# Attention's normalising in blocks of eight heads instead of four, with buffers by block

## The chip, the cores and the metric

The kernel runs on one core of a Trainium2 chip. The metric is device time in microseconds (us), the median of the runs shown.

## What is computed

The reference chains an attention with sinks and a sliding window and two MLPs, all in float32. Only its core stands here.

```python
# attention: 2 batches, 8 heads, 768 positions, head dimension 64; 4 sinks, window 128
scores = scale * np.matmul(q, k.transpose(0, 1, 3, 2))
keep = is_sink | in_window
scores = np.where(keep, scores, -1e9)
a = np.exp(scores - max(scores))
a = a / (sum(a) + 1e-9)
x = np.matmul(a, v)          # reshaped to 1536 tokens x 512
h = x @ w_in                 # first MLP, 512 -> 2048 -> 512
x = np.where(h > 0, h, np.exp(np.minimum(h, 0)) - 1) @ w_out
h = x @ w2_in                # second MLP
out = (h - np.tanh(h)) @ w2_out
```

## The kernel before

Every operation is first recorded by `Plan` (lines 42 to 400) and then put into an order by a list scheduler, which works with costs and waiting times written into the class. Among operations that are ready on an engine it takes the one with the highest rank. For a kind of work that has an entry in `DUE` (line 62) the rank comes from a due time in us, a first value plus a second one times the number of the group, chunk or step; smaller is earlier. Kinds without an entry are ranked by the length of the work that hangs on them. `PICK` (line 69) says for operations that several engines could do which of them may. `BONUS` is what PE gives for staying in its tile mode, `MARGIN` what another engine must be faster by before an operation is left to it. Where PE would be idle in the schedule's reckoning before the first MLP ends its first step, `idle` (line 588) is put in, a filler matmul that is of no other use. As the order is fixed when the kernel is built, the queues of all engines run in that order. Nearly all instructions carry line 400, several matmuls recorded together line 168, fillers line 591.

Attention works on 12 chunks of 128 positions; six make up one batch. A group is half a chunk's heads, four, so there are 24. In `attention` (line 799) a group runs `scores` twice, for two heads each: PE writes scores into two banks (`b_sc`, two in all), DVE adds the mask and takes the maximum (into `nm_all`), ACT makes exponentials and their sums (`sm_all`). Then `norm` (line 724) adds 1e-9 to the four sums, takes reciprocals and scales the four heads' rows. `sink_T` (line 736) is for chunks that see the sinks apart from their window: it copies the sinks' weights, splits them into a rounded part and a remainder, and transposes them on PE. `pair_T` transposes two heads' weights, and an eviction brings them to `arena`. When both groups of a chunk are done, `PV` (line 771) multiplies by the values and splits the result into `xhi` and `xlo`, which the MLPs read. Rows are 128 columns wide in the first chunk of a batch, 256 in the second, 264 in the other four.

The first MLP begins beside attention, in blocks of 256 tokens with three pieces of its weights (`PHASES`, line 437; each piece has an in and an out half, six halves in all); all later stages work on 512 tokens. `w_split` (line 854) loads a half's 64-bit words, narrows them (line 829) and splits them into a rounded part and a remainder in `w`, by work on ACT, DVE and POOL. Two buffers `raw` serve the loads of the first weights. Loads are issued on SP.

Buffers that the change touches: `r_a` (line 530, weights of attention, three of four heads each), `r_aT` (line 532, transposed pairs, eight), `r_as` and `r_asT` (lines 534 and 535, sinks' weights and their transposes, one and two).

Of the kernel before, what the change touches and what calls it, by code (L numbers as in the profile page):

```python
# [41 lines left out]
class Plan:  # L42
# [16 lines left out]
    BONUS, MARGIN = 2030.75, 5520.33  # L59
# [11 lines left out]
        ("norm", "tensor_scalar", 264, False): ("DVE",), ("T", "copy", 64, False): ("POOL",),  # L71
        ("late w", "tensor_scalar", 512, False): ("DVE",), ("late ew", "tensor_tensor", 512, False): ("DVE",),
        ("T", "tensor_tensor", 32, False): ("DVE",), ("late ew", "copy", 512, False): ("ACT",),
        ("c", "tensor_copy", 128, False): ("POOL",), ("w", "tensor_scalar", 512, False): ("POOL",),
        ("late w", "tensor_tensor", 512, False): ("DVE",), ("late out", "copy", 512, True): ("DVE",),
        ("w", "tensor_tensor", 512, False): ("DVE",), ("T", "copy", 256, True): ("ACT",),
        ("late w", "copy", 512, False): ("DVE",), ("T", "copy", 512, True): ("ACT",),
        ("out", "copy", 512, True): ("ACT",), ("x", "copy", 512, True): ("ACT", "DVE"),
        ("norm", "tensor_scalar", 128, False): ("DVE",), ("norm", "tensor_scalar", 256, False): ("DVE", "POOL"),
        ("w", "copy", 512, False): ("ACT", "DVE", "POOL"), ("z", "copy", 512, False): ("DVE",),  # L80
        ("ew", "tensor_tensor", 256, False): ("DVE",),
# [322 lines left out]
def tile_sink_attention__two_mlps(  # L404
# [52 lines left out]
    def copy(out, in_):  # L457
        ways = [(V_, "tensor_copy"), (S_, "copy")]
        if in_.space != PSUM:
# [21 lines left out]
             F32R: arena_p.tile([P, 2464], F32R, name="arena_r")}  # L481
# [45 lines left out]
    KS, NS, QB, VB, AB, TB = 144, 3, 2, 4, 3, 8  # L527
    r_q = Ring("att", (HP, P), F32, QB)
    slots = carve("att", (NS, HP, KS))
    r_a = Ring("att", (4, KW), F32, AB)  # L530
# [3 lines left out]
    r_as = Ring("att", (3, 4, MAXSINK), F32R)  # L534
    r_asT = Ring("att", (P,), F32R, 2)
# [152 lines left out]
    def scores(g, pr):  # L688
# [4 lines left out]
        if pr == 0:  # L693
            a_t[g] = r_a()
# [16 lines left out]
        for e in range(2):  # L711
            j = place(g, e) + pr
            col = 4 * g + j
            a = a_t[g][:, j, 0:n]
# [9 lines left out]
    def norm(g):  # L724

        plan.tag = ("norm", g)
        n = width((g // 2) % NI)
        r = sm_all[:, 4 * g:4 * g + 4]
        ts(out=r, in0=r, scalar1=1e-9, scalar2=None, op0=ALU.add)
        V_.reciprocal(out=r, in_=r)  # L730
        for j in range(4):
            a = a_t[g][:, j, 0:n]
            plan.either((G_, "tensor_scalar"), (V_, "tensor_scalar"), out=a, in0=a, scalar1=r[:, j:j + 1],
                        scalar2=None, op0=ALU.mult)

    def sink_T(g):
        plan.tag = ("T", g)
        if (g // 2) % NI < 2:
            return
        a = a_t[g][:, :, P:P + MAXSINK]  # L740

        s = r_as()
        copy(s[:, 1:3], a.unsqueeze(1).to_broadcast([P, 2, 4, MAXSINK]))
        sub(None, s[:, 0], a, s[:, 1].bitcast(F32))
        tr = b_tu(P)[0:3 * S4]
        T_.matmul(
            out=tr, lhsT=s.rearrange("p a h s -> p (a h s)").bitcast(F32), rhs=ident,
            is_transpose=True, start=True, stop=True,
        )
        aS_t[g] = r_asT()[0:3 * S4]  # L750
        copy(aS_t[g], tr)

    def pair_T(g, pr):
# [4 lines left out]
        a = a_t[g]  # L758
# [432 lines left out]
```

## Time and profile before

| | us |
|---|---|
| median of 3 runs | 637.05 |
| lowest and highest | 636.72, 637.23 |
| the profiled execution | 636.36 |
| its span, first to last instruction | 634.6 |
| PE busy in it | 627.1 |
| DVE busy | 431.9 |
| ACT busy | 278.6 |
| POOL busy | 30.8 |

The clock granted to PE was 0.998 of full speed in the mean. PE is TensorE's matmuls, PEld its weight loads, DVE VectorE, ACT ScalarE, POOL GpSimd, SP the engine that issues DMAs. The ends of matmuls are modelled and overlap, so a group's mean time is longer than the step from one matmul to the next. A line of the timeline that merges several instructions gives the time from the first start to the last end; an instruction may start before the end that is shown for the one ahead of it.

### The profile page before, as it was taken

The page shows a single profiled execution, that of the slowest core. Times are in us where ns is not written, and L with a number is a line of the kernel's source. Part 1 is how long each engine was busy: PE and PEld are TensorE (multiplying, and loading weights), DVE is VectorE, ACT ScalarE, POOL GpSimd, SP SyncE. Part 2 cuts the span into 40 slices and gives each one's busy share as a digit, 9 for nine tenths or more (in the row PEclk, how much of TensorE's full clock was granted, in tenths as well). Part 3 has the DMA queues.
Part 4 walks back from the last instruction along what each step waited for, and adds up shares of the span by engine and source line. Part 5 has one row for each costly group of instructions (what it writes and reads, how often), then busy time and mean ns, then how long its engine had stood idle before and what let it go on. Part 6 is the DMA issues. An engine that isn't in the chain of part 4 may idle for free.

```text
span 634.6 us, 9256 instructions
## 1 busy us (share of the span) xinstructions
PE 627.1 (99%) x3430; PEld 514.5 (81%) x3430; DVE 431.9 (68%) x1061; ACT 278.6 (44%) x615; POOL 30.8 (5%) x41
## 2 busy tenths in 40 slices
PE   9999999999999999999999999999999999999996
PEld 6677877899888888888888888888888888888885
DVE  6999999999824479943459998367974553423232
ACT  5788887875533345533445453223422222222220
POOL 3631020100000000000000000000000000000000
PEclk9999999999999999999999999999999999999999
DMA  6543444345500122430012243011220000001012
GB/s 212 172 162 121 130 162 133 99 139 165 165 1 0 35 66 68 132 100 0 1 34 67 74 158 116 17 40 59 70 66 2 2 0 1 0 1 66 2 66 72
DMA packets 22005, 47.21 MB, mean 74 GB/s; under 512 B 2240, under 2 KB 9408, under 8 KB 21952
## 3 DMA queue, kind: packets, MB, share of 16 engines
q1 hardware_dynamic: 21952, 46.54, 23.7%
q8 instruction: 29, 0.48, 0.3%
q14 instruction: 24, 0.20, 0.1%
HBM read 43.39 MB, written 3.15 MB: 73 GB/s over the span
## 4 chain that ended last, share of the span: by engine, by line
PE 82%; DVE 13%; DMA 2%; POOL 1%; SPq 1%; issue 1%; ACT 0%; DVEq 0%; POOLq 0%
PE bank L400 79%; DVE arena L400 7%; DVE t L400 3%; PE bank L168 2%; DVE arena_r L400 1%; DVE w L400 1%; DMA raw<-in_moe_w_in_dram 1%; DVE xlo L400 1%; SPq L400 1%; POOL t L400 1%; DMA arena<-in_kq_dram 1%; DVE sm_all L400 1%; POOL arena_r L400 0%; DVE xhi L400 0%; ACT arena L400 0%
## 5 line engine op out<-in xcount | busy, mean ns | idle before, releaser
L400 PE MATMUL bank<-xhi,w 128*128 128x512 f32 (+1 forms) x840 | 250.7, 373 | 0.0
L400 PEld LDWEIGHTS bank<-xhi,w 128*128 128x128 f32 x840 | 154.6, 188 | 28.7 <-issue 1.6
L400 PE MATMUL bank<-arena_r,w 128*128 128x512 f32 (+1 forms) x684 | 158.8, 358 | 0.0
L400 PE MATMUL bank<-w,arena_r 128*128 128x512 f32 (+1 forms) x594 | 154.4, 383 | 0.0
L400 PE MATMUL bank<-xlo,w 128*128 128x512 f32 (+1 forms) x420 | 148.2, 373 | 0.0
L400 ACT CAST arena_r<-arena 128x512 fp32r<-128x512 f32 (+1 forms) x96 | 57.9, 603 | 194.2 <-PE bank L400 192.1
L400 PEld LDWEIGHTS bank<-arena_r,w 128*128 128x128 f32 x684 | 116.5, 189 | 19.3 <-issue 0.9
L400 DVE TENSOR_TENSOR arena_r<-arena,arena_r 128x512 fp32r<-128x512 f32 (+3 forms) x123 | 71.4, 582 | 89.1 <-PE bank L400 42.8
L400 PEld LDWEIGHTS bank<-w,arena_r 128*128 128x128 f32 x594 | 109.3, 188 | 22.1
L400 ACT ACTIVATE arena<-bank 128x512 f32<-128x512 f32 (+1 forms) x105 | 57.9, 560 | 101.0 <-PE bank L400 97.5
L400 PEld LDWEIGHTS bank<-xlo,w 128*128 128x128 f32 x420 | 79.0, 188 | 14.6 <-issue 1.1
L400 DVE TENSOR_TENSOR arena<-bank,arena 128x512 f32<-128x512 f32 (+1 forms) x65 | 42.4, 677 | 38.2 <-ACT arena L400 31.8
L168 PE MATMUL bank<-arena 128*64 128x128 f32 (+3 forms) x544 | 55.3, 327 | 0.5 <-DVE nm_all L400 0.4
L400 ACT ACTIVATE arena<-arena,nm_all 128x264 f32<-128x264 f32 (+2 forms) x96 | 46.8, 491 | 15.6 <-DVE nm_all L400 14.9
L400 DVE SCALAR_TENSOR_TENSOR arena<-arena,bank 128x512 f32<-128x512 f32 (+1 forms) x57 | 33.9, 596 | 22.0 <-ACT arena L400 22.0
L400 ACT ACTIVATE arena<-arena 128x512 f32<-128x512 f32 (+1 forms) x73 | 42.5, 587 | 8.1 <-DVE w L400 6.6
L168 PEld LDWEIGHTS bank<-arena 128*64 128x64 f32 (+1 forms) x544 | 34.7, 154 | 11.1 <-issue 4.3
L400 DVE SCALAR_TENSOR_TENSOR t<-raw,t 128x512 uint32<-128x512 uint32 x54 | 37.2, 688 | 0.2
L400 DVE CUSTOM_DVE_ANT_0 arena<-bank,arena 128x264 f32<-128x264 f32 (+2 forms) x96 | 35.1, 398 | 0.4 <-PE bank L168 0.2
L400 ACT COPY arena<-bank 128x512 f32<-128x512 f32 (+1 forms) x52 | 27.5, 544 | 3.2 <-PE bank L168 3.2
L400 DVE TENSOR_SCALAR t<-t 128x512 f32<-128x512 f32 (+1 forms) x64 | 27.1, 425 | 2.0 <-POOL t L400 1.1
L168 PE MATMUL bank<-ident,arena 128*128 128x128 f32 x176 | 27.6, 281 | 0.2 <-DVE xlo L400 0.2
(67 smaller groups left out, 408.8 us busy)
## 6 DMA issues: line engine op xcount, KB each, us to landing
raw<-in_moe_w_in_dram SPq DMA_DIRECT2D x20, 512.0 KB, 3.7
raw<-in_moe_w_out_dram SPq DMA_DIRECT2D x20, 512.0 KB, 3.8
arena<-in_moe_w_in_dram SPq DMA_DIRECT2D x12, 512.0 KB, 3.6
arena<-in_moe_w_out_dram SPq DMA_DIRECT2D x12, 512.0 KB, 3.6
arena<-in_kq_dram SPq DMA_DIRECT2D x22, 256.0 KB, 3.4
arena<-in_v_dram SPq DMA_DIRECT2D x12, 256.0 KB, 3.4
out_dram<-part SPq DMA_DIRECT2D x8, 256.0 KB, 2.2
out_dram<-arena SPq DMA_DIRECT2D x3, 256.0 KB, 2.5
```

Source lines behind the costliest of these rows:

```text
L168: eng.matmul(**kw)
L400: real(*self.ops[n][3], **self.ops[n][4])
```

## The change

The buffers of attention's weights hold a whole chunk, eight heads, and there are two of them. `norm` and `sink_T` run once a chunk, behind both groups' scores: one addition and one reciprocal for eight sums, then eight scalings; one subtraction for the sinks' weights of both groups, two transposes into one bank recorded together, one eviction. The four `pair_T` and `PV` follow. Transposed pairs have six buffers in place of eight, the transposed sinks one of double size. The constants of the plan are others: due times, the engines that may do an operation, `BONUS` and `MARGIN`.

```diff
--- before.py
+++ after.py
@@ -56,29 +56,31 @@
     TOP = 640e3
     WINDOW, ENOUGH, IDLE = 3413.3, 3100.0, (109.2, 256.0)
     SWITCH = (196.0, 95.0)
-    BONUS, MARGIN = 2030.75, 5520.33
+    BONUS, MARGIN = 10109.72, 5963.27
 
     HOLD = {}
     DUE = {
-        "c": (-2246.58, 70.043), "score": (-751.72, 15.580), "ew": (169.97, 10.912), "lkq": (-825.49, 29.089),
-        "norm": (31.65, 0.041), "lw": (-323.61, 20.339), "w": (-51.16, 95.951), "end": (1519.18, -106.955),
-        "x": (-392.68, 18.828), "pv": (89.97, 9.529), "in": (76.02, 17.601), "out": (207.21, 11.159),
-        "kq": (-189.70, 22.587), "T": (23.13, 10.469), "ok": (444.48, 24.538), "lv": (48.72, 3.987),
+        "c": (-2406.72, -14.630), "score": (-1413.68, 28.549), "ew": (331.51, 0.606), "lkq": (-1382.77, 27.576),
+        "norm": (-507.50, -6.572), "lw": (-1164.05, 68.531), "w": (2009.13, 142.798), "end": (1067.44, -87.300),
+        "pv": (-462.76, 5.811), "in": (81.51, 14.384), "out": (102.53, 20.095), "T": (-367.90, 8.180),
+        "x": (-151.46, 6.200), "z": (192.47, 20.402), "late ew": (-512.87, 6.303), "lv": (-62.63, 13.646),
+        "ok": (4.72, 0.000),
     }
 
     PICK = {
         ("T", "copy", 128, True): ("ACT",), ("ew", "copy", 256, False): ("ACT", "DVE"),
-        ("norm", "tensor_scalar", 264, False): ("DVE",), ("T", "copy", 64, False): ("POOL",),
-        ("late w", "tensor_scalar", 512, False): ("DVE",), ("late ew", "tensor_tensor", 512, False): ("DVE",),
-        ("T", "tensor_tensor", 32, False): ("DVE",), ("late ew", "copy", 512, False): ("ACT",),
-        ("c", "tensor_copy", 128, False): ("POOL",), ("w", "tensor_scalar", 512, False): ("POOL",),
-        ("late w", "tensor_tensor", 512, False): ("DVE",), ("late out", "copy", 512, True): ("DVE",),
-        ("w", "tensor_tensor", 512, False): ("DVE",), ("T", "copy", 256, True): ("ACT",),
-        ("late w", "copy", 512, False): ("DVE",), ("T", "copy", 512, True): ("ACT",),
-        ("out", "copy", 512, True): ("ACT",), ("x", "copy", 512, True): ("ACT", "DVE"),
-        ("norm", "tensor_scalar", 128, False): ("DVE",), ("norm", "tensor_scalar", 256, False): ("DVE", "POOL"),
-        ("w", "copy", 512, False): ("ACT", "DVE", "POOL"), ("z", "copy", 512, False): ("DVE",),
-        ("ew", "tensor_tensor", 256, False): ("DVE",),
+        ("norm", "tensor_scalar", 264, False): ("DVE", "POOL"), ("T", "copy", 64, False): ("ACT", "DVE"),
+        ("late w", "tensor_scalar", 512, False): ("DVE",),
+        ("late ew", "tensor_tensor", 512, False): ("DVE", "POOL"), ("T", "tensor_tensor", 32, False): ("DVE",),
+        ("late ew", "copy", 512, False): ("DVE",), ("c", "tensor_copy", 128, False): ("POOL",),
+        ("w", "tensor_scalar", 512, False): ("POOL",), ("late w", "tensor_tensor", 512, False): ("DVE",),
+        ("late out", "copy", 512, True): ("ACT",), ("w", "tensor_tensor", 512, False): ("DVE",),
+        ("T", "copy", 256, True): ("DVE",), ("late w", "copy", 512, False): ("DVE", "POOL"),
+        ("T", "copy", 512, True): ("ACT",), ("out", "copy", 512, True): ("ACT",),
+        ("x", "copy", 512, True): ("ACT",), ("norm", "tensor_scalar", 128, False): ("DVE",),
+        ("norm", "tensor_scalar", 256, False): ("DVE",), ("w", "copy", 512, False): ("ACT", "DVE"),
+        ("z", "copy", 512, False): ("DVE",), ("ew", "tensor_tensor", 256, False): ("DVE",),
+        ("T", "tensor_tensor", 64, False): ("DVE", "POOL"),
     }
 
     def __init__(self, tc):
@@ -478,7 +480,7 @@
 
 
     arena = {F32: arena_p.tile([P, 14336], F32, name="arena"),
-             F32R: arena_p.tile([P, 2464], F32R, name="arena_r")}
+             F32R: arena_p.tile([P, 2560], F32R, name="arena_r")}
     bank = [banks_p.tile([P, 512], F32, name=f"bank{n}") for n in range(8)]
     top_of = {}
 
@@ -524,15 +526,15 @@
 
     gsA = Ring("att", (2, 256), F32R, 3)
 
-    KS, NS, QB, VB, AB, TB = 144, 3, 2, 4, 3, 8
+    KS, NS, QB, VB, AB, TB = 144, 3, 2, 4, 2, 6
     r_q = Ring("att", (HP, P), F32, QB)
     slots = carve("att", (NS, HP, KS))
-    r_a = Ring("att", (4, KW), F32, AB)
+    r_a = Ring("att", (8, KW), F32, AB)
     masks = carve("att", (4, KW))
     r_aT = Ring("att", (2, 2, P), F32, TB)
     r_v = Ring("att", (H, D), F32, VB)
-    r_as = Ring("att", (3, 4, MAXSINK), F32R)
-    r_asT = Ring("att", (P,), F32R, 2)
+    r_as = Ring("att", (2, 3, 4, MAXSINK), F32R)
+    r_asT = Ring("att", (2, P), F32R, 1)
     r_vsink = Ring("att", (HP, P), F32R)
     eA = Ring("att", (256,), F32, 2)
     part2 = carve("late", (4, 512))
@@ -690,8 +692,8 @@
         plan.tag = ("score", g)
         c, half = divmod(g, 2)
         i, o = c % NI, c % NS
-        if pr == 0:
-            a_t[g] = r_a()
+        if pr == 0 and half == 0:
+            a_t[c] = r_a()
         p = 2 * half + pr
         n = width(i)
         mm, S = [], []
@@ -711,7 +713,7 @@
         for e in range(2):
             j = place(g, e) + pr
             col = 4 * g + j
-            a = a_t[g][:, j, 0:n]
+            a = a_t[c][:, 4 * half + j, 0:n]
             V_.tensor_tensor_reduce(
                 out=a, in0=S[e][:, 0:n], in1=masks[:, mi, 0:n], scale=-SCALE, scalar=3.0e38,
                 op0=ALU.add, op1=ALU.min, accum_out=nm_all[:, col:col + 1],
@@ -721,41 +723,44 @@
                 bias=nm_all[:, col:col + 1], accum_out=sm_all[:, col:col + 1],
             )
 
-    def norm(g):
-
-        plan.tag = ("norm", g)
-        n = width((g // 2) % NI)
-        r = sm_all[:, 4 * g:4 * g + 4]
+    def norm(c):
+
+        plan.tag = ("norm", 2 * c + 1)
+        n = width(c % NI)
+        r = sm_all[:, 8 * c:8 * c + 8]
         ts(out=r, in0=r, scalar1=1e-9, scalar2=None, op0=ALU.add)
         V_.reciprocal(out=r, in_=r)
-        for j in range(4):
-            a = a_t[g][:, j, 0:n]
+        for j in range(8):
+            a = a_t[c][:, j, 0:n]
             plan.either((G_, "tensor_scalar"), (V_, "tensor_scalar"), out=a, in0=a, scalar1=r[:, j:j + 1],
                         scalar2=None, op0=ALU.mult)
 
-    def sink_T(g):
-        plan.tag = ("T", g)
-        if (g // 2) % NI < 2:
+    def sink_T(c):
+        plan.tag = ("T", 2 * c + 1)
+        if c % NI < 2:
             return
-        a = a_t[g][:, :, P:P + MAXSINK]
+        a = a_t[c].rearrange("p (g h) k -> p g h k", g=2)[:, :, :, P:P + MAXSINK]
 
         s = r_as()
-        copy(s[:, 1:3], a.unsqueeze(1).to_broadcast([P, 2, 4, MAXSINK]))
-        sub(None, s[:, 0], a, s[:, 1].bitcast(F32))
-        tr = b_tu(P)[0:3 * S4]
-        T_.matmul(
-            out=tr, lhsT=s.rearrange("p a h s -> p (a h s)").bitcast(F32), rhs=ident,
-            is_transpose=True, start=True, stop=True,
-        )
-        aS_t[g] = r_asT()[0:3 * S4]
-        copy(aS_t[g], tr)
+        for g in range(2):
+            copy(s[:, g, 1:3], a[:, g].unsqueeze(1).to_broadcast([P, 2, 4, MAXSINK]))
+        sub(None, s[:, :, 0], a, s[:, :, 1].bitcast(F32))
+        tr = b_tu(2, P)[0:3 * S4]
+        plan.many([
+            dict(out=tr[:, g], lhsT=s[:, g].rearrange("p a h s -> p (a h s)").bitcast(F32), rhs=ident,
+                 is_transpose=True, start=True, stop=True)
+            for g in range(2)
+        ])
+        t = r_asT()[0:3 * S4]
+        copy(t, tr)
+        aS_t[2 * c], aS_t[2 * c + 1] = t[:, 0], t[:, 1]
 
     def pair_T(g, pr):
 
         plan.tag = ("T", g)
         c = g // 2
         i = c % NI
-        a = a_t[g]
+        a = a_t[c][:, 4 * (g % 2):4 * (g % 2) + 4]
         tr = b_tu(2, 2, P)
         c0, c1 = slice(0, P), slice(P, 2 * P) if i == 1 else s1
         cols = (c1, c0) if i != 1 and c % NS == 0 else (c0, c1)
@@ -810,11 +815,11 @@
                 load_v(c + 1)
             scores(g, 0)
             scores(g, 1)
-            norm(g)
-            sink_T(g)
-            pair_T(g, 0)
-            pair_T(g, 1)
             if half:
+                norm(c)
+                sink_T(c)
+                for k in range(4):
+                    pair_T(2 * c + k // 2, k % 2)
                 PV(c)
```

## Rows read from the trace of the kernel before

**Rows 1.** Busy time by stage: length, then busy us (instructions) per engine, clock, DMA.
```profile
0.00:30.00 30.00, 28.70 (x219) 18.35 (x221) 25.13 (x113) 19.29 (x62) 14.87 (x19) 1.00 0.60 187
30.00:109.00 79.00, 78.82 (x693) 61.60 (x689) 77.71 (x308) 64.87 (x205) 13.97 (x18) 1.00 0.45 142
109.00:152.90 43.90, 43.86 (x402) 40.52 (x403) 43.29 (x131) 32.57 (x83) 2.00 (x4) 1.00 0.45 139
152.90:634.60 481.70, 475.71 (x2122) 394.08 (x2120) 285.82 (x513) 161.90 (x269) 0.00 (x0) 1.00 0.16 50
```

**Rows 2.** Chain that ended last, in order of time: start us, us, engine, tile written.
```profile
108.39 0.61 DVE xlo L400
109.04 0.66 PE bank L168 x4
```

**Rows 3.** Fillers (line 591): all of them, those until 30 us, two windows, one series.
```profile
L591 PE MATMUL bank<-const-bfloat16-1.0 x122: 272/273/418, 0.8 to 40.4; 128*16 128x256 bf16 x122
...
L591 PE MATMUL bank<-const-bfloat16-1.0 128*16 128x256 bf16 x117 | 16.7, 288 | 0.8 <-PEq L1145 0.8
...
10.00:20.00 10.00, 5.29 (x41) 3.18 (x39) 1.00 0.65 221
20.00:30.00 10.00, 4.21 (x29) 2.27 (x29) 1.00 0.55 176
...
17.32 1.83 PE L591 MATMUL bank<-const-bfloat16-1.0 128*16 128x256 bf16 x15
```

**Rows 4.** DVE by time, 50 to 80 us: start us, us, operation, shapes, count.
```profile
52.51 0.16 DVE L400 TENSOR_SCALAR sm_all<-sm_all 128x4 f32<-128x4 f32 x1
52.58 0.41 DVE L400 TENSOR_TENSOR arena_r<-arena,arena_r 128x256 fp32r<-128x256 f32 x1
52.92 0.17 DVE L400 RECIPROCAL sm_all<-sm_all 128x4 f32<-128x4 f32 x1
53.01 0.38 DVE L400 SCALAR_TENSOR_TENSOR arena<-arena,bank 128x256 f32<-128x256 f32 x1
53.31 1.15 DVE L400 TENSOR_SCALAR arena<-arena,sm_all 128x264 f32<-128x264 f32 x4
...
56.62 0.18 DVE L400 TENSOR_TENSOR arena_r<-arena,arena_r 128x32 fp32r<-128x32 f32 x1
56.73 0.68 DVE L400 TENSOR_TENSOR w<-t,w 128x512 fp32r<-128x512 f32 x1
```

**Rows 5.** Groups by shape, DVE until 109 us, last ACT whole span: busy, mean ns.
```profile
L400 DVE SCALAR_TENSOR_TENSOR t<-raw,t 128x512 uint32<-128x512 uint32 x24 | 16.6, 692 | 0.1
L400 DVE TENSOR_SCALAR arena<-arena,sm_all 128x264 f32<-128x264 f32 x48 | 14.3, 348 | 0.0
L400 DVE TENSOR_TENSOR w<-t,w 128x512 fp32r<-128x512 f32 x11 | 7.5, 678 | 0.0
...
L400 DVE TENSOR_SCALAR arena<-arena,sm_all 128x256 f32<-128x256 f32 x9 | 3.6, 431 | 0.0
...
L400 DVE CAST xhi<-bank 128x512 fp32r<-128x512 f32 x3 | 2.0, 681 | 0.0
...
L400 ACT CAST arena_r<-arena 128x512 fp32r<-128x512 f32 (+1 forms) x96 | 57.9, 603 | 194.2 <-PE bank L400 192.1
```

**Rows 6.** Head by time: DVE, then POOL, then PE, between 16 and 32 us.
```profile
16.46 0.69 DVE L400 SCALAR_TENSOR_TENSOR t<-raw,t 128x512 uint32<-128x512 uint32 x1
...
19.09 0.41 DVE L400 CUSTOM_DVE_ANT_0 arena<-bank,arena 128x256 f32<-128x256 f32 x1
...
19.77 0.68 DVE L400 TENSOR_TENSOR w<-t,w 128x512 fp32r<-128x512 f32 x1
...
18.00 3.24 POOL L400 TENSOR_SCALAR arena<-arena,sm_all 128x256 f32<-128x256 f32 x3
...
29.23 2.63 PE L168 MATMUL bank<-arena 128*64 128x128 f32 x36
...
31.88 0.50 PE L400 MATMUL bank<-xhi,w 128*128 128x256 f32 x2
```

## Prediction, made before the changed kernel was run

> **What bounds the kernel now.** I read the busy time by stage first [rows 1]. In it the reader is to see where DVE is full: 25.1 of the first 30 us, 77.7 of the next 79, still full from 109 to 152.9, and 59% (285.8 of 481.7 us) after that. PE looks full in every stage, but ends of matmuls are modelled and fillers count as work, so this column alone decides nothing. The chain that ended last does: in order of time it runs nearly wholly through DVE until 108.39 us, through PE from 109.04 us on [rows 2]. So the time is what the front takes on DVE, plus PE's work from 109 us on, which the change leaves as it is.
>
> Then I ask how much PE really idles in the front, since only that can be won. 117 fillers lie in the first 30 us, 41 of them from 10 to 20 and 29 from 20 to 30 us; 15 in a row take 1.83 us, 0.12 each, so all 117 take 14 us [rows 3]. From 30 to 109 us only 5 fillers are left (122 in all, from the count in [rows 3]), and the better measure is PEld: weight loads are busy 61.6 of 79 us there (78%), against 40.5 of 43.9 (92%) in the stage behind it, where PE never leaves the chain [rows 1]. Were the mix of matmuls the same, PE would idle 79 x (1 - 78/92) = 12 us; the lower bound is the 5 fillers, 0.6 us. I take 5 us. **Ceiling: 14 us in the head, some 5 us after it.**
>
> **The change, part by part.** Terms are of the profiled run (span 634.6 us, 636.36 with what lies around it). That is 0.7 us under the median of 637.05, and I subtract what is saved from the median.
>
> Reciprocals. 24 additions and 24 reciprocals of four columns become 12 and 12 of eight. They last 0.16 and 0.17 us, but on a full engine what counts is when the next instruction starts: the addition at 52.51 is followed at 52.58, the reciprocal at 52.92 at 53.01 [rows 4]. Twelve pairs at 0.16 us are 1.9 us; by the durations, as the upper bound, 12 x 0.33 = 4.0. The four more columns I take at nothing, beside a scaling's 264.
> By the Trainium skill ("VectorE: DVE Perf Modes", section on the TRN2 errata) an instruction carries a fixed term that it measures at about 150 cycles and that is exposed between instructions. An estimate from that page, 24 x 0.156, would make this term 3.7 us. The rows agree with the figure as a duration and disagree as a step from start to start; by the rows it is 1.9.
>
> Sinks' weights. 16 subtractions of 32 columns become 8 of 64. One steps by 0.11 us (56.62 to 56.73 [rows 4]); eight fewer and eight somewhat longer give 0.7 us (0 to 0.9). The 16 transposes stay; the 16 evictions behind them on ACT become 8, off the chain. The 16 copies of 64 columns leave POOL for ACT or DVE: at the same 0.11 us, half of them on DVE, +0.9 us (0 to 1.8). Reciprocals and sinks: when the chain turns to PE at 109 us, 48 of the 64 scalings of full width are done [rows 5] and all 32 narrower ones, five sixths, so 2.6 x 5/6 = 2.2 us less and 0.9 x 5/6 = 0.8 more.
>
> Where operations may run. Eight evictions of 256 columns (chunks 0 and 6) go from ACT to DVE; an operation of that width steps by 0.34 us (52.58 to 52.92 [rows 4]): +2.7. Three casts to xhi leave DVE, 0.68 us each [rows 5], 0.08 less from start to start as at 52.58: -1.8. The seven 256-column scalings on POOL come back to DVE; four of 264 columns take 1.15 us at 53.31 and one 0.35, so one more takes 0.27 [rows 4, 5]: +1.9. In return POOL may take 264-column scalings. It took 7 of the 16 narrower ones (9 ran on DVE [rows 5]); now eight come at once and each takes POOL 1.1 us (three in 3.24 [rows 6]), in which DVE does four. I reckon with two in eight, 12 ahead of 109 us: -3.2. DVE's neighbours give some back: its own nine of 256 columns, some beside POOL's, took 431 ns in the mean, the longer ones 348 [rows 5]; at 0.08 for each of 12, +1.0. Three casts of weights leave POOL (+0.5), later ones may go there (-0.8).
> The Trainium skill ("GPSIMD Engine Reference", section Key points) says that POOL shares its SBUF interfaces with VectorE and contends with its two-port modes. The 431 ns agree; did the contention eat this whole gain, the sum would be 2.2 us worse.
>
> The sum on DVE is -2.2 + 0.8 + 2.7 - 1.8 + 1.9 - 3.2 + 1.0 + 0.5 - 0.8 = **-1.1 us**. Bounds: +2.7 if POOL takes no scaling (+2.2), all sinks' copies fall to DVE (+0.8) and no later cast moves (+0.8); -5.8 if reciprocals count by duration (-1.7), POOL takes half of the scalings (-2.2) and no sinks' copy falls to DVE (-0.8). DVE is full and on the chain, so it counts one to one until the 5 us are used up.
>
> Order. Due times change too: splitting of the first weights gets due 2009 and later, behind everything in attention, and splitting the sinks gets a due of its own behind the value products. The place to read this is the head [rows 6]. Chunk 1's last two score reductions run on DVE from 19.09 on, its value products start at 29.23, the first MLP product at 31.88. Ahead of those reductions stand passes over weights from 16.46 us on; POOL scales three heads one after another from 18.00 to 21.24. With all scalings of 256 columns on DVE (eight at 0.27: 2.2 us) and weights and sinks behind them, chunk 1 could be ready some 5 us earlier, an estimate from these rows. But the product needs a weight as well; its first half got its remainder at 19.77 [rows 6], and these passes now come last. I take 2 us (0 to 5): of the 29 fillers from 20 to 30 us, 3.5 us, a little over half turn into products.
>
> Blocks of eight speak against it: scaling of the first four heads (1.15 us) used to go beside scores of the last four, and so did their transposes; at least 1.2 us a chunk, for the two chunks that the first product needs, 2.4 us. The 5 us above less these is 2.6, another reason to take 2. After 32 us MLP products cover the longer path; without them it would cost 1.2 us in each of the ten other chunks. Attention's buffer grows from 12 heads to 16, so scores may run further ahead; six transposed pairs in place of eight are still a chunk and a half. With one buffer of transposed sinks, its copy waits for the value products of the chunk before, and behind it on ACT (64.9 of 79 us busy [rows 1]) queue exponentials; this wait is new, I take it at nothing, and at 0.5 us in each of eight chunks if it bites.
>
> Late operations. Casts of the MLP's hidden values leave ACT for DVE, 96 of them, nearly all behind 109 us [rows 5]. At no more than 0.4 us each, DVE goes from 286 to some 320 of 482 us. PE's products cover that, so nothing; without cover 0.4 us a step. No load's code changes. Raw buffers refill when weights have been split, so loads of weights come later on SP, and keys' loads behind them wait less; I take nothing.
>
> **Sum:** 637.05 - 1.1 - 2.0 = **634.0 us**, rounded.
>
> **Rivals.** (a) More is won: with attention ahead, PE's 5 us after 30 us vanish and 3 us of fillers with them: 637.05 - 8 = 629. For it: two merges and the remainder of each weight take 16.6 + 7.5 us of DVE ahead of 109 us [rows 5], and some could wait. Against: PE's products need just these.
> (b) Slower, by starved weights. The last of the six halves of the first three weights gets its remainder at 56.73 us [rows 4], and a first block of tokens needs all six. Strictly behind attention they get only holes in a DVE that has none after 30 us [rows 1]. Where PE has attention alone, from 10 to 30 us, 70 fillers of 0.12 us are 42% of the time [rows 3]. If the last half comes some 25 us later and PE idles half as much as in the head, this costs 25 x 0.21 = 5 us: 637.05 - 1.1 + 5 = 641. It decides if that half is ready after about 70 us.
> (c) No change that counts: DVE's sum is +1, inside its bounds, and the head gains 1 us: 637. That the blocks don't become eight is no rival: the diff builds them with plain loops.
>
> **How the numbers follow.** Less than about 0.2% (1.3 us) can't be told from no change here. The forecast's case, 632 to 635.8, gets 0.37, (a) 0.20, (c) 0.17, (b) 0.26: faster 0.57, same 0.17, slower 0.26. The forecast's own bounds are 637.05 - 5.8 - 2 = 629.3 and, without gain in the head, 637.05 + 2.7 = 639.8. The range 628 to 641 takes in these and the prices of (a) and (b), and leaves out about 0.05 below and 0.13 above, where starving costs more.
>
> **What would show it.** Right: 12 additions and 12 reciprocals; the first MLP product ahead of 30 us; fewer than 105 fillers; a chain that turns from DVE to PE ahead of 107 us; POOL with some 16 scalings. Wrong: that sixth half after 70 us (b); fillers up by 30; a first product later than 33 us; more DVE work up to the turn than now; or a wait of PE behind DVE after 153 us, which I have at nothing.

## The result: 1.2% slower, nearly all of it lost ahead of 161 us

The changed kernel took 644.13 us in the median (643.08 to 646.28, 4 runs), the kernel before, run beside it, 636.99. The ratio is 1.0119, with a 95% interval of 1.0107 to 1.0131: 7.1 us slower where 3 us faster was forecast, and outside the range of 628 to 641. The profiled execution took 643.08 us, with a span of 641.3; before it was 636.36 and 634.6.

Busy time by stage of the changed kernel, in the columns and stages of [rows 1]:

```profile
0.00:30.00 30.00, 29.24 (x226) 18.72 (x228) 24.27 (x116) 18.55 (x61) 6.03 (x12) 1.00 0.60 184
30.00:109.00 79.00, 76.06 (x671) 59.30 (x665) 78.66 (x278) 63.14 (x192) 29.65 (x28) 1.00 0.47 144
109.00:152.90 43.90, 41.53 (x374) 37.50 (x375) 40.60 (x119) 30.93 (x80) 12.89 (x10) 1.00 0.48 144
152.90:641.30 488.40, 482.30 (x2172) 399.94 (x2170) 304.48 (x527) 118.45 (x201) 78.28 (x62) 1.00 0.16 49
```

Three things are to be seen. PE, which idled hardly at all after 30 us, now has holes: 2.9 us of 79 and 2.4 of 43.9. DVE is a little less busy in the head (24.27 us, 25.13 before) and fuller from 30 to 109 (78.66, 77.71). The granted clock is 1.00 in all rows, as before, so it isn't the clock.

The waits of PE between 30 and 150 us (what waited for what: us in total, times, longest), all there are. The kernel before:

```profile
PE bank L168 <- DVE xlo L400: 0.2, 1, 0.2
```

The changed kernel:

```profile
PE bank L170 <- DVE arena_r L402: 1.8, 2, 1.2
PE bank L170 <- DVE nm_all L402: 1.2, 2, 0.6
PE bank L170 <- POOL arena_r L402: 0.9, 2, 0.7
PE bank L402 <- DVE xlo L402: 0.7, 1, 0.7
PE bank L402 <- DVE arena L402: 0.3, 1, 0.3
PE bank L170 <- DVE xlo L402: 0.2, 1, 0.2
```

That is 0.2 us against 5.1. Fillers come on top (line 593 now, windows as in [rows 3], the last one from 30 us on):

```profile
10.00:20.00 10.00, 4.68 (x37) 2.78 (x36) 1.00 0.68 233
20.00:30.00 10.00, 4.65 (x36) 2.67 (x34) 1.00 0.59 157
30.00:130.00 100.00, 1.50 (x9) 0.72 (x9) 1.00 0.46 140
```

A filler that reaches over the edge of a window is counted in both; by their starts there are 34 from 20 to 30 us (29 before) and 9 behind it (5), and over the whole run 127, 122 before. The chain no longer turns to PE at 109 us for good, as in [rows 2]; it comes back and leaves DVE at 133 us only (start us, us, what):

```profile
109.07 1.86 PE bank L170 x10
...
114.30 3.74 POOL arena L402 x2
...
125.54 0.33 POOL arena L402
125.87 3.70 issue
129.57 0.95 POOL arena L402
130.55 0.40 ACT arena_r L402 x2
...
131.04 0.23 DVE arena_r L402
...
133.25 0.66 PE bank L170 x4
...
139.60 10.51 PE bank L402 x86
```

"issue" is time in which the engine waited for nothing that the profile shows: POOL's first scaling, begun at 125.54, is not done before 129.57.

To place the loss in time I use PE's order of work. The first MLP's first step works on 256 tokens, what follows on 512, and the two overlap a little; so I look for the first product of 512 tokens and the last ones of 256. The kernel before:

```profile
152.93 0.40 PE L400 MATMUL bank<-xhi,w 128*128 128x512 f32 x1
...
155.48 1.35 PE L400 MATMUL bank<-arena_r,w 128*128 128x256 f32 x10
```

The changed kernel:

```profile
156.06 0.40 PE L402 MATMUL bank<-xhi,w 128*128 128x512 f32 x1
...
156.53 4.46 PE L402 MATMUL bank<-arena_r,w 128*128 128x256 f32 x36
```

The last product of the first step starts at 156.54 us before, with 10 products of 512 tokens ahead of it, and at 160.71 after, with 2; taking 0.23 us off for each of these (four take 0.91 us), the first step is done some 154.3 and 160.3 us in, 6.0 us later. Of these the waits between 30 and 150 us are 4.9 and the five more fillers, 0.12 us each, 0.6. DVE's last instruction starts at 628.65 before and 635.36 after, 6.7 later, so 0.7 us are lost behind the first step. They lie at 386 us, between two steps, where weight loads wait for DVE's additions (from 156 us on; the kernel before has no such wait):

```profile
PEld bank L402 <- DVE arena L402: 1.0, 3, 0.4
```

The measure of the experiments below, "late by", is the last start of the first step less 0.23 us for each product of 512 tokens ahead of it, against the kernel before.

### The profile page after: what moved, and what is told of

The parts are those of the page before. It is cut to its first block, busy times and chain, and to the rows that moved or that the text cites. A ratio compares the mean times of both kernels' runs of the same rounds, so it can differ in the third digit from the quotient of the medians.

```text
span 641.3 us, 9226 instructions
## 1 busy us (share of the span) xinstructions
PE 629.1 (98%) x3435; PEld 515.5 (80%) x3435; DVE 448.0 (70%) x1035; ACT 231.1 (36%) x531; POOL 126.8 (20%) x111
## 4 chain that ended last, share of the span: by engine, by line
PE 80%; DVE 16%; issue 1%; POOL 1%; DMA 0%; SPq 0%; ACT 0%; DVEq 0%; POOLq 0%
PE bank L402 74%; DVE arena L402 8%; PE bank L170 5%; DVE t L402 3%; DVE w L402 2%; DVE arena_r L402 2%; PE bank L593 1%; POOL arena L402 1%; DVE xlo L402 0%; DMA arena<-in_v_first_dram 0%; SPq L402 0%; DVE sm_all L402 0%; POOL arena_r L402 0%; ACT arena L402 0%; DVE nm_all L402 0%
## 5 line engine op out<-in xcount | busy, mean ns | idle before, releaser
L402 PE MATMUL bank<-xhi,w 128*128 128x512 f32 (+1 forms) x840 | 253.9, 374 | 0.3 <-DVE arena L402 0.3
L402 PE MATMUL bank<-arena_r,w 128*128 128x512 f32 (+1 forms) x684 | 166.7, 358 | 0.0
L402 PE MATMUL bank<-xlo,w 128*128 128x512 f32 (+1 forms) x420 | 144.3, 373 | 0.7 <-DVE xlo L402 0.7
L402 PEld LDWEIGHTS bank<-arena_r,w 128*128 128x128 f32 x684 | 120.2, 189 | 20.4 <-issue 1.9
L402 POOL TENSOR_TENSOR arena_r<-arena,arena_r 128x512 fp32r<-128x512 f32 (+1 forms) x36 | 52.5, 1460 | 319.7 <-DVE arena_r L402 151.7
L402 DVE CAST arena_r<-arena 128x512 fp32r<-128x512 f32 (+3 forms) x102 | 41.6, 409 | 85.3 <-PE bank L402 84.4
L402 DVE TENSOR_TENSOR arena_r<-arena,arena_r 128x512 fp32r<-128x512 f32 (+3 forms) x79 | 48.2, 611 | 29.7 <-PE bank L402 26.6
L402 POOL TENSOR_SCALAR arena<-arena,sm_all 128x264 f32<-128x264 f32 x19 | 25.2, 1336 | 39.6 <-DVE sm_all L402 20.5
L402 DVE TENSOR_SCALAR arena<-arena 128x512 f32<-128x512 f32 (+2 forms) x60 | 29.7, 498 | 3.9 <-ACT arena L402 3.3
```

The source lines that it names most:

```text
L402: real(*self.ops[n][3], **self.ops[n][4])
```

## The experiments

On each chip the kernel before ran beside them; its medians lay from 636.71 to 636.86, and the differences are to the one beside.

| kernel | median, us | ratio, 95% interval | to before, us | its traced run to before's, us | first step late by |
|---|---|---|---|---|---|
| changed kernel | 644.1 | 1.0119 (1.0107 to 1.0131) | +7.1 | +6.7 | 6.0 |
| blocks of eight, old constants (e4) | 640.0 | 1.0052 (1.0035 to 1.0069) | +3.2 | +3.2 | 3.2 |
| the same, due times moved up to 6 us (e18) | 640.2 | 1.0056 (1.0039 to 1.0073) | +3.4 | +3.7 | 3.6 |
| norm by chunk only (e20) | 641.5 | 1.0074 (1.0057 to 1.0091) | +4.7 | +6.8 | 6.4 |
| sinks by chunk only (e19) | 639.4 | 1.0043 (1.0027 to 1.0060) | +2.6 | +3.0 | 3.0 |
| blocks, first two chunks in fours (e10) | 638.7 | 1.0028 (1.0019 to 1.0038) | +2.0 | +2.4 | 2.4 |
| blocks, new due times, old choice of engines (e11) | 642.3 | 1.0095 (1.0082 to 1.0108) | +5.5 | +5.9 | 5.9 |
| changed kernel, its scalings off POOL (e1) | 642.1 | 1.0082 (1.0061 to 1.0103) | +5.3 | +5.2 | 5.2 |
| changed kernel, due times moved up to 2 us (e17) | 642.4 | 1.0093 (1.0076 to 1.0109) | +5.6 | +5.8 | 5.7 |
| old blocks, all new constants (e5) | 642.1 | 1.0083 (1.0066 to 1.0099) | +5.3 | +5.8 | 3.8 |
| before, new due times (e7) | 637.9 | 1.0021 (1.0011 to 1.0031) | +1.1 | +1.3 | 1.3 |
| before, new choice of engines (e8) | 640.2 | 1.0048 (1.0031 to 1.0065) | +3.5 | +4.1 | 3.9 |
| before, new BONUS and MARGIN (e9) | 636.7 | 0.9996 (0.9986 to 1.0005) | 0.0 | +0.7 | 0.7 |
| before, 256 columns on DVE (e12) | 641.6 | 1.0072 (1.0059 to 1.0084) | +4.8 | +5.5 | 5.1 |
| before, the other new entries (e13) | 641.7 | 1.0079 (1.0066 to 1.0093) | +4.8 | +4.9 | 4.2 |
| before, own order, 19 scalings on POOL (e6) | 637.0 | 1.0005 (0.9995 to 1.0014) | +0.2 | +0.4 | 0.4 |
| before, own order, 8 evictions on DVE (e14) | 638.6 | 1.0028 (1.0017 to 1.0039) | +1.7 | +1.5 | 1.5 |
| before, due times moved up to 2 us (e15) | 637.0 | 1.0006 (0.9996 to 1.0015) | +0.1 | +0.2 | 0.2 |
| before, due times moved up to 6 us (e16) | 637.9 | 1.0019 (1.0009 to 1.0028) | +1.1 | +0.9 | 0.9 |

The last two columns are of one run each, the traced one, and belong together (before: 636.36 us). In e20 that run is 1.7 us above the median; the other three lie from 641.30 to 641.64. Of most losses nearly all is in the first step. The largest exception is e5, where 1.9 of 5.8 us lie behind DVE's last instruction (3.9 us late), where results are stored; why, isn't shown. Nine runs fell into none of the ranges set down for them: e1, e4, e6, e10, e11, e12, e13, e16 and e20.

"Own order" means that the recorded order is kept and only the engine of the named instructions is replaced as they are issued, so no other instruction changes its place. No kernel beats the one before.

**Blocks against constants.** The changed kernel with the old `DUE`, `PICK`, `BONUS` and `MARGIN`:

```diff
-    BONUS, MARGIN = 10109.72, 5963.27
+    BONUS, MARGIN = 2030.75, 5520.33
...
+        ("ew", "tensor_tensor", 256, False): ("DVE",), ("T", "tensor_tensor", 64, False): ("DVE",),
```

The lines of `DUE` and the others of `PICK` go back likewise and aren't shown.

> Blocks of eight and their buffers, but due times, choice of engines, BONUS and MARGIN of the kernel before (the new shape of the sinks' subtraction goes to DVE). Theory P and a theory that the new due times cost the time: 635 to 638, as before or a little less, since 2 us of DVE's small operations go. Theory S (the block of eight itself, by its longer path): 641 to 645.

+3.2 us, and PE hardly waits (0.2 us from 30 to 150 us); it gets fillers instead, 149 where [rows 3] have 122, at 0.12 us each 3.2 us. Then the other way round, the old blocks with the constants of the change:

> Groups of four as before, but with the constants of the changed kernel. Theory P and the theory of due times: 641 to 646, since POOL gets scalings here too. Theory S: 636 to 638, as before.

+5.3, of which 3.8 in the first step. Both halves cost, and 3.2 + 5.3 is more than the whole 7.1, so the two can't be added.

**Which part of the blocks.** One kernel (e19) makes sums, reciprocals, scalings and transposes in fours and the sinks' weights by chunk, the other (e20) the reverse; both have attention's buffers by chunk and the old constants. The second of them, against the kernel before (its buffers are not shown):

```diff
-            norm(g)
-            sink_T(g)
-            pair_T(g, 0)
-            pair_T(g, 1)
             if half:
+                norm(c)
+                sink_T(2 * c)
+                sink_T(2 * c + 1)
+                for k in range(4):
+                    pair_T(2 * c + k // 2, k % 2)
                 PV(c)
```

> Old constants; sums, reciprocals and scalings of eight heads at once and transposes behind them, sinks' weights by group of four as before with two buffers. Theory that the longer path is that of the scalings: 639.5 to 641 us, some 150 fillers, the first MLP product past 34 us. Rival, that the sinks make it: 636 to 637.5 (12 additions and 12 reciprocals fewer).

> Old constants; sums, scalings and transposes of pairs in groups of four as before, sinks' weights once a chunk with one buffer of double size, buffers by chunk as in the change. Theory that the longer path is that of the scalings: 636 to 637.5 us (8 subtractions, 8 evictions and 8 instructions of transposes fewer). Rival, that the single buffer of transposed sinks holds the copy back: 639 to 640.

Each part costs alone, +4.7 and +2.6, and they don't add up to the blocks' +3.2. What norm by chunk does is seen on DVE in the head, kernel e20 (start us, us, operation; in brackets the wait before it):

```profile
9.36 0.29 DVE L400 CUSTOM_DVE_ANT_0 arena<-bank,arena 128x128 f32<-128x128 f32 x1 [0.91 <-PE bank L168]
...
10.76 0.29 DVE L400 CUSTOM_DVE_ANT_0 arena<-bank,arena 128x128 f32<-128x128 f32 x1 [0.89 <-PE bank L168]
...
13.07 2.24 DVE L400 TENSOR_SCALAR arena<-arena,sm_all 128x128 f32<-128x128 f32 x8
```

and in the kernel before:

```profile
8.33 0.17 DVE L400 RECIPROCAL sm_all<-sm_all 128x4 f32<-128x4 f32 x1
8.54 0.87 DVE L400 TENSOR_SCALAR arena<-arena,sm_all 128x128 f32<-128x128 f32 x4
9.42 0.29 DVE L400 CUSTOM_DVE_ANT_0 arena<-bank,arena 128x128 f32<-128x128 f32 x1
```

Before, reciprocal and scaling of the first four heads fill the time in which PE makes the next scores. In blocks there is nothing to do then: DVE stands still, and the eight scalings stand in one piece behind. The sums of DVE's waits until 30 us for PE's banks, and for the exponentials on ACT ahead of the sums, in the kernel before:

```profile
DVE sm_all L400 <- ACT arena L400: 1.4, 2, 0.7
...
DVE arena L400 <- PE bank L168: 0.2, 1, 0.2
```

with norm by chunk (e20):

```profile
DVE arena L400 <- PE bank L168: 3.3, 4, 0.9
...
DVE sm_all L400 <- ACT arena L400: 0.7, 1, 0.7
```

and in the changed kernel:

```profile
DVE arena L402 <- PE bank L170: 2.3, 3, 0.9
...
DVE sm_all L402 <- ACT arena L402: 0.7, 1, 0.7
```

Together that is 1.6 us before, 4.0 in e20 and 3.0 in the changed kernel: blocks save one of the two waits for ACT and pay more for it in waits for PE. In the first 12 us DVE is busy 7.7 us before, 5.4 in e20, 6.4 in the changed kernel and in e4, so 1.3 to 2.3 us of it are gone by then. In e20 the value products of chunk 1 start at 33.15 us (29.23 in [rows 6]) and the first MLP product at 36.13 (31.88), in e4 at 31.57 and 34.55. If that is the cause, taking the first two chunks out of the blocks gives it back:

```diff
-            if half:
+            if c < 2:
+                norm(c, 4 * half, 4 * half + 4)
...
+            elif half:
                 norm(c)
```

> Blocks of eight with the constants of the kernel before, as the run that took 3.2 us more, but the first two chunks are normalised and transposed in groups of four again. Theory H (the block's longer path costs only in the head, where the first MLP product waits for chunks 0 and 1): 635 to 637.5, the 3.2 us gone, and some of the 2 us of small operations won. If the path costs in every chunk: 639 to 640.

The remainder of chunk 1 (`xlo`), the last that its value products leave behind, comes at 32.53 us before and at this time with blocks (e4):

```profile
35.34 0.69 DVE L400 TENSOR_TENSOR xlo<-bank,xhi 128x512 fp32r<-128x512 f32 x1
```

with the first two chunks in fours (e10), where the second line is chunk 2's (45.43 before):

```profile
32.31 0.68 DVE L400 TENSOR_TENSOR xlo<-bank,xhi 128x512 fp32r<-128x512 f32 x1
...
49.90 0.68 DVE L400 TENSOR_TENSOR xlo<-bank,xhi 128x512 fp32r<-128x512 f32 x1
```

So chunk 1's delay of 2.8 us is the block's: it goes wholly with the block. The time does not follow: 1.2 us come back of 3.2; DVE's waits for PE are 0.5 us and the fillers 130. The other 2.0 us arise in the later chunks. The delay comes anew with chunk 2, the first in a block, 4.5 us, and chunk 4's remainder stands at 72.90 us (66.91). Which wait does that isn't shown. For the sinks' part alone I have little more than that it costs. It fell into the range of its rival, the single buffer: ACT stood still 1.9 us ahead of its eight copies into that buffer (0.6 ahead of 16 in the kernel before), so it may have a share in e19. In the changed kernel DVE makes these copies and stood still 0.0 us ahead of them. Chunks 0 and 1, which have no sinks apart, are 0.75 and 0.8 us late in e19 already (19.24 and 33.34, before 18.49 and 32.53), so the buffers by chunk or the other order may have a share in it; a kernel with the buffers alone was not run, nor one with a second buffer of transposed sinks for the blocks.

**The constants one by one**, in the kernel before:

> The kernel before with the due times alone of the changed kernel; choice of engines, BONUS and MARGIN as before. Old structure with all new constants took 5.3 us more than before. Theory D (weights last: products of the MLP come late, and PE waits in the order for what DVE does behind attention): 640 to 642, nearly all of the 5.3. Theory K (the choice of engines) and theory M (BONUS, which keeps PE in a tile mode): 636 to 638.

> The kernel before with the changed kernel's choice of engines alone (evictions of 256 columns on DVE, casts to xhi on ACT, sinks' copies on ACT or DVE, POOL allowed for full-width scalings and for late work). Theory K: 640 to 642. Theories D and M: 636 to 638.

> The kernel before with BONUS 10109.72 and MARGIN 5963.27 alone. Theory M (PE keeps to its tile mode for longer, so that what DVE waits for comes later): 639 to 642. Theories D and K: 636 to 638.

+1.1, +3.5 and nothing. Due times that put weights behind attention did not bring chunk 1 forward: its remainder comes at 34.69 us, 2.2 later than before. I then halved the choice of engines, on one side the entries of 256 columns, on the other the rest:

```diff
-        ("w", "tensor_tensor", 512, False): ("DVE",), ("T", "copy", 256, True): ("ACT",),
+        ("w", "tensor_tensor", 512, False): ("DVE",), ("T", "copy", 256, True): ("DVE",),
...
-        ("norm", "tensor_scalar", 128, False): ("DVE",), ("norm", "tensor_scalar", 256, False): ("DVE", "POOL"),
+        ("norm", "tensor_scalar", 128, False): ("DVE",), ("norm", "tensor_scalar", 256, False): ("DVE",),
```

> The kernel before with two entries of the new choice of engines only: evictions of 256 columns and scalings of 256 columns on DVE alone (chunks 0, 1, 6 and 7). The prediction costed these at +2.7 and +1.9 us of DVE, five sixths and more of it ahead of the turn of the chain. Theory that these two make most of the choice's +3.5 us, since half of them lie in the head where the first chunk is waited for: 639 to 640.5 us, more fillers than 122 in the first 40 us. Rival, that DVE has room for them where they fall: 636.8 to 637.5.

> The kernel before with all other entries of the new choice of engines: scalings of 264 columns on DVE or POOL, sinks' copies on ACT or DVE, casts to xhi on ACT alone, casts of weights off POOL, casts of late hidden values on DVE, late subtractions and casts also on POOL. Together with the run of the two 256-column entries it should make about the whole choice's +3.5 us. Theory that those two are most of it: 636.8 to 638 here. Rival, that POOL's scalings beside DVE and the late work on POOL are most of it: 639 to 640.5.

Either half costs more (+4.8) than the whole (+3.5). Such shares can't be added: each list of constants makes another order. The other way is to keep the order. The eight evictions alone, issued on DVE in place:

> The kernel before in its own order, with the eight evictions of 256 columns (chunks 0 and 6) issued on DVE instead of ACT; nothing else moves. The prediction's term for this is +2.7 us of DVE, counted one to one on the path. Theory that the term is right: 638.5 to 639.5 us. Rival, that the four of chunk 0 lie in a head where DVE's later work waits for other things, and the four of chunk 6 count: +1.3, 638.1. Rival, that nothing follows (ACT's exponentials come sooner in exchange): 636.8.

+1.7, not +2.7. Chunk 0's remainder moves from 18.49 to 18.64 us only, so its four evictions cost 0.15; chunk 5's, 76.85 before, moves to 77.68 and chunk 8's from 108.30 to 109.79. Behind chunk 6's four, 1.3 us more: where DVE is full the term is near one to one, in the head it is not. In e12, where the order was made anew, the same chunk 0 is ready at 21.70.

**POOL's scalings**, in place both ways: 19 of 64 given to POOL in the kernel before, and the changed kernel's 19 given back to DVE.

```diff
-            for _, n, real in self.order:
+            for _, n, real in map(self.swap, self.order):
```

`swap`, not shown, puts the other engine's instruction into the same place.

> The kernel before in its own order; 19 of its 64 full-width scalings are issued on POOL instead of DVE at the same place (the last of each four, and three more). Theory P: DVE's scalings beside them get longer, transposes wait for POOL, 639 to 643. If POOL's help is worth what I reckoned (19 x 0.27 us less 0.08 each): 633 to 636.

> The changed kernel in its own order, instruction for instruction; only the 19 full-width scalings that POOL did are issued on DVE at the same place of the order. Theory P (POOL's scalings slow DVE beside them and end late, and PE waits behind that): 19 scalings at 0.27 us come to DVE, but its other 45 fall from 464 ns in the mean to about 350, so its work stays as it was and the waits for POOL go: 639 to 641 us, 3 to 5 less than the changed kernel. Theory O (it is the new order by due times, or the longer path of a block of eight): 644 as before, or up to 649 if POOL's help was worth its 5 us.

Nothing gained in the kernel before; 1.8 us gained by giving them back in the changed one (+5.3 for +7.1; 2.0 by the medians, which are of two chips). The groups of scalings of 264 columns (busy us, mean ns), the changed kernel's on POOL and on DVE:

```profile
L402 POOL TENSOR_SCALAR arena<-arena,sm_all 128x264 f32<-128x264 f32 x19 | 25.2, 1336 | 39.6 <-DVE sm_all L402 20.5 <-ACT arena L402 13.2 <-PE bank L402 5.9
L402 DVE TENSOR_SCALAR arena<-arena,sm_all 128x264 f32<-128x264 f32 x45 | 18.6, 464 | 0.0
```

DVE's in e1, where it does all 64:

```profile
L402 DVE TENSOR_SCALAR arena<-arena,sm_all 128x264 f32<-128x264 f32 x64 | 20.0, 368 | 0.0
```

and in e6, the kernel before with 19 on POOL; [rows 5] have 348 ns:

```profile
L400 DVE TENSOR_SCALAR arena<-arena,sm_all 128x264 f32<-128x264 f32 x45 | 16.6, 418 | 0.0
```

19 scalings fewer on DVE free 20.0 - 18.6 = 1.4 us of it in the changed kernel, 2.4 in the kernel before (19.0 for its 64), where 19 x 0.29 = 5.5 were moved ([rows 4]: four in 1.15). And what waits for POOL waits long (changed kernel, by time):

```profile
125.54 4.97 POOL L402 TENSOR_SCALAR arena<-arena,sm_all 128x264 f32<-128x264 f32 x2 [2.61 <-DVE sm_all L402]
125.56 1.41 DVE L402 TENSOR_SCALAR arena<-arena,sm_all 128x264 f32<-128x264 f32 x5
...
128.36 0.41 DVE L402 TENSOR_SCALAR t<-t 128x512 f32<-128x512 f32 x1
...
130.55 0.39 ACT L402 CAST arena_r<-arena 128x64 fp32r<-128x64 f32 x2 [2.31 <-POOL arena L402]
...
131.04 0.23 DVE L402 TENSOR_TENSOR arena_r<-arena,arena_r 128x64 fp32r<-128x64 f32 x1 [2.27 <-ACT arena_r L402]
...
131.32 0.42 PE L170 MATMUL bank<-ident,arena_r 128*96 128x128 f32 x2 [1.24 <-DVE arena_r L402]
```

DVE has finished five scalings when POOL has not done one; the sinks' copy of the whole chunk waits for POOL's last, and through it DVE, which stands still from 128.77 us to 131.04, and PE. I take it that the blocks make this price, as in e6 a scaling on POOL holds up the sinks of four heads and not of eight; no run separates it.

**How much any new order costs.** Moving due times a little leaves the work as it is and changes which of two near-equal operations goes first (in e16 two operations move from DVE to ACT by it).

> The kernel before with the first value of each due time moved by a random amount of up to 2 us; instructions and engines stay, their order changes in places. Theory that a new order costs by itself: 638 to 641 us, the loss ahead of 153 us. Rival, that small shifts of order cancel and the differences found so far belong to the edits: 636.4 to 637.4.

> As the run before it, with up to 6 us and other random amounts. Theory that a new order costs by itself: 638 to 642 us. Rival, that it doesn't: 636.4 to 637.6.

> The changed kernel with the first value of each due time moved by a random amount of up to 2 us. Theory that orders differ by chance and that the changed kernel's is one of many: 641 to 646 us, to either side of 644.1. Rival, that the loss belongs to the blocks and the choice of engines: 643.5 to 644.7.

> Blocks of eight with the old constants and each due time's first value moved by a random amount of up to 6 us. The blocks alone gave 640.0 with unmoved ones. Theory that the +3.2 us of the blocks is their longer path: 639 to 641. Rival, that it is the chance of one order: outside of 638.5 to 641.5, to either side.

0.1 and 1.1 us for the kernel before, -1.7 for the changed one, +0.2 for the blocks. So some 1 to 2 us may be the chance of one order, as far as four moved orders tell. The blocks' +3.2, which came at both of their orders, and the whole +7.1 are more than that. The due times' +1.1 and the 1.2 us that e10 gives back can't be told from it; for e10 its rows speak, not its time. A last one takes one step out of the change, the old choice of engines with the rest kept:

> Blocks of eight with the new due times, BONUS and MARGIN, but the old choice of engines (the 64-column subtraction, which it does not know, on DVE). Theory that the shares add: blocks alone +3.2 and new due times +1.1 make 636.8 + 4.3 = 641.1 us. Rival, that the due times fit the blocks (first chunks ahead of weights are worth something only where eight are made at once): at or under the 640.0 of blocks with the old constants. Rival, that the due times clash with the blocks and the choice of engines is innocent in this structure: 643 to 644, no better than the changed kernel.

642.3 us. So there is a path on which each step was measured: 636.9 before, 640.0 with blocks (+3.1), 642.3 with new due times, BONUS and MARGIN too (+2.3), 644.1 with the new choice of engines (+1.8, of the size of what POOL's scalings cost there). Of the last two steps each is near what an order may cost by chance, so what the new constants cost beside the blocks, some 4 us, is measured as a sum, and its parts are not shown.

## Why the prediction was wrong, point by point

**"Order", -2.0 us, failed, and with it the forecast.** It rested on chunk 1 being ready 5 us earlier, and held the block's longer path, 2.4 us, as already contained. The gain did not come: the value products of chunk 1 start at 29.14 us instead of 29.23, the first MLP product at 31.90 instead of 31.88, and behind it PE puts in 7 fillers until chunk 1's remainder is there at 33.11 (32.53 before):

```profile
29.14 2.63 PE L170 MATMUL bank<-arena 128*64 128x128 f32 x36
...
31.90 0.38 PE L402 MATMUL bank<-xhi,w 128*128 128x256 f32 x1
```

The longer path did come: +3.2 us as a whole for the blocks. Against the sentence "After 32 us MLP products cover the longer path" speak the 4.5 us by which chunk 2 is late in e10 and the 2.0 us that stay there. In the changed kernel itself the first product is on time, and what I had at nothing is PE's waiting behind it, 5.1 us for attention's results between 30 and 150 us.

**"DVE is full and on the chain, so it counts one to one" failed in the head.** I read 25.1 of 30 us as full. The missing 5 are waits, and the four-head scaling was what kept them small: 0.2 us for PE's scores, 2.3 to 3.3 with blocks; with the wait for ACT, which blocks halve, 1.6 and 3.0 to 4.0. There the four-head scaling filled a wait; merged into the block it left the wait open. The sum of operations was near: until 109 us DVE is busy 102.9 us, 102.8 before, where I had -1.1; its waits and their place were not in the sum.

**Reciprocals and sinks, -2.2 and +0.8.** The counts came: 12 additions (164 ns) and 12 reciprocals (194 ns) instead of 24 and 24 (0.16 and 0.17 us in [rows 4]). No run shows a gain from them; each part alone lost more than it could save. The wait for the single buffer of transposed sinks, taken at nothing, does not show in the changed kernel.

**POOL's scalings, -3.2 + 1.0.** Number right (19, some 16 foreseen), size wrong. DVE's mean went from 348 to 464 ns, 0.12 each for all 45, not 0.08 for twelve, and the wait for POOL was left out. The sum named this case: "did the contention eat this whole gain, the sum would be 2.2 us worse". In the kernel before it did just that (e6, +0.2); in blocks it cost some 2 us more, by the wait for POOL.
The Trainium skill ("SBUF — State Buffer", section "Who interferes with whom") says that VectorE in a two-port mode and GpSimd exclude each other for whole instructions and do not share. The rows of 125.5 us agree: five DVE scalings at 0.28 us each, undisturbed, and a POOL scaling that took 4 us and ended 0.8 us behind DVE's last instruction of that stretch. "Perfetto Trace Analysis", section "Optimizing Scalar/DVE Operations", of the same skill says that moving work between those two might not help; e6 bears it out.

**Evictions, +2.7** measured +1.7, right in kind: one to one where DVE is full, 0.15 us for the four in the head.

**Late operations, nothing:** 0.7 us, PE's wait for DVE at 386 us, the last of the signs that should show the forecast wrong. With the old choice of engines (e11) it is gone. DVE rose from 285.8 to 304.5 us behind 153 us, POOL from 0 to 78.3.

**Rivals.** (b) ended nearest, but not for its reason. The sixth half came 9.7 us later:

```profile
66.47 0.68 DVE L402 TENSOR_TENSOR w<-t,w 128x512 fp32r<-128x512 f32 x1
```

which is ahead of the 70 us from which (b) decides; PE waited for attention's results (`arena_r`, `nm_all`, `xlo`), not for weights, in the rows above. In e7, with the due times alone, that half came at 62.35 and the price was 1.1 us. The rival I lacked was the block's own path as a loss: I had its price (1.2 us a chunk) and let a hoped-for gain swallow it. Of what should show the forecast right, the counts and POOL's scalings came; the first product ahead of 30 us, fewer than 105 fillers (127) and a turn ahead of 107 us did not. Of what should show it wrong, the first three did not come (the sixth half at 66.47 us, five fillers more, a first product at 31.90): none of them names PE's waits in mid-attention.

## What to carry to other kernels

Before merging two half-size steps, look at what the first one ran beside: if it filled a wait of its engine, the merged step saves its fixed cost and opens the wait; in the first 12 us of this kernel that took 1.3 to 2.3 us of DVE. A gain and a loss on the same path are two cases with chances of their own, not one net number. Where a planner makes the order anew, measure an edit in place as well, and move its due times a little to see what chance does: parts that cost 4.8 us each cost 3.5 together.

## What was not expected of the hardware

One instruction on POOL was stretched by what DVE did beside it: POOL's scalings of 128x264 took 0.94 us at the least, 1.12 in the median and 4.05 at the longest (x19, changed kernel). The longest began at 125.54 us; DVE ran scalings and passes over weights without a break from 125.56 to 128.77, and 0.82 us behind that, less than the shortest scaling takes, it was done.

```profile
L402 POOL TENSOR_SCALAR arena<-arena,sm_all x19: 941/1117/4046, 29.7 to 129.6; 128x264 f32<-128x264 f32 x19
```
